# Sparse attention with a maxout layer behind it on one core: the last 136 of 822 tasks in another order

## The chip, the core and the metric

The kernel runs on one core of a Trainium2 chip. The metric is the device time of one execution in microseconds (us); of several executions the median is taken. Three runs of the kernel before gave 164.91, 164.93 and 164.22 us, a median of 164.91 us. A profiled execution stands beside them.

## The reference

Two stages, from float32 inputs to a float32 output of 3072 x 512. Batch is 4, heads 8, sequence 768, head size 64.

```python
# attention: each query sees the keys within 15 positions, and one summary key per block of 32
k_sum = k.reshape(B, H, nb, block, D).max(axis=3)
v_sum = v.reshape(B, H, nb, block, D).mean(axis=3)
scores_l = scale * q @ k^T, masked to |i - j| < 16
scores_s = scale * q @ k_sum^T + log(32)
a = softmax(concat[scores_l, scores_s])
attn = a @ concat[v, v_sum]
# maxout: x is attn as 3072 x 512
out = maximum(x @ w1, x @ w2) @ w_out
```

## The kernel before

The kernel does not compute the maxout in the reference's form. Since max(h1, h2) = h1 + relu(h2 - h1), it computes relu(x @ (w2 - w1)) @ w_out + x @ (w1 @ w_out). The difference of the weights and the product w1 @ w_out are made once.

The work is a list of 822 tasks. A task is one step on one tile: a group of matmuls, an exp, a copy, a load, a store. The program creates the tasks batch by batch; then three strings in `CFG` say everything about their placing. `CFG["engines"]` has one letter for each task: T is TensorE (PE), D is VectorE (DVE), A is ScalarE (ACT), P is GpSimd (POOL), S is the queue of SyncE (SP). `CFG["order"]` is a list of task numbers in the order in which they are emitted, and each engine runs its own tasks in that order. `CFG["slots"]` has one digit for each buffer, which says which tile of its ring it gets. All three are written out by hand or by a search outside the program; `Plan.run` (lines 122 to 132) only reads them. Waits follow from the buffers: a task waits for the writers of what it reads, and for the last users of the tile that it writes into. A store or a copy that waits holds up whatever stands behind it on its engine.

The labels name a task by its numbers, and these are needed to follow the steps:

- "scores", "exp", "mask", "values", "inv", "x" and "dxt" carry batch b, head pair hp (0 or 2) and group grp (0 to 2). "scores 302" is batch 3, head pairs 0 and 1, group 2. "values" has one more digit, the head pair within the two. A group is 256 rows of the sequence.
- "dxt" (lines 595 to 599) is a DMA transpose from SP: it turns the attention output x into the tile xt, from which the maxout reads. "x" (line 590) is the DVE step before it: it divides by the row sum that "inv" (line 587) inverted.
- "hidden" and "relu" (lines 674 to 694) carry b, grp and a quarter n of the hidden layer: eight 256-column matmuls, and the relu behind them on ACT or DVE.
- "outx", "outg0", "outg1", "copy out" and "store" (lines 702 to 733) carry b, grp and a half u of 128 rows. "outx" multiplies xt by w1 @ w_out, "outg0" and "outg1" the halves of the relu's output by w_out, each with four matmuls. Then the tile is copied out of its bank, by ACT or DVE, and stored by the queue of SP or ACT. Tile 320 is cut by columns into 256 + 128 + 128.

A hidden or outx task of batch 3 needs both of its group's transposes, dxt 30g and dxt 32g. The banks of the matmul outputs (eight, ring "banks") are shared by scores, values, hidden and out; a task that takes a bank waits for the step that emptied it.

The output rows of a tile are shifted by 16 (line 727: `at = grp * GT + u * 128 + 16`). So the tile of grp 2, u 1 ends 16 rows beyond its batch, and its last 16 rows are the batch's first: it takes two stores (lines 729 and 731). All other tiles take one.

Before the change, the end of the list is, on the engines that matter:

- PE: values 3200, 3021, 3201, 3020, 3000, 3001; hidden 312, 310, 313, 311; outx 310, outx 311, outg0 311, outx 320 (128), outg1 311; hidden 320, outg0 310, hidden 322, 323, 303, 301, 300, 302, 321; outg1 310, outx and outg0 320 (128), outx and outg0 301, outg1 320 (128), outg1 301, outx and outg0 300, the rest of 320, outg1 300; outx, outg0 and outg1 321.
- DVE, behind mask 300: inv 320, inv 302, x 302, x 320, inv 300, relu 310, 312, 311, x 300, relu 313, copy out 311, relu 300, 322, copy out 310, relu 302, copy out 320 (128) twice.
- ACT, behind exp 301: copy out 211, copy out 221, store 221, exp 302, exp 300, relu 323, store 200, relu 301, store 211, relu 320, 321, 303, copy out 220, copy out 301, store 301, store 311, copy out and store 320 (256), copy out 300, copy out 321, store 321.
- SP, behind the last transpose of keys and queries: store 201, 111, 100, dxt 321, 301, 322, 302, 320, 300, store 011, 210, 310, 220, 121, 320 (128) twice, store 300.

Of the kernel before, what the change touches and what calls it, by code (L numbers as in the profile page):

```python
# [27 lines left out]
DAPAPTADADAPAPDATATDDPDADDTATDDPDPDPSDSDDPDPDSASADDPDTADTTDDSTADTTDDSTADTTDDSTADTTDDSTADTTDDSTADTTDDSSSSDSSSDSSSDSSSDP  # L28
ADPAAATAPPDDDPPAPSASDDDPPASASDDAPPPSDSDDADPDSDSADDPDTADTTDDSTADTTDDSTADTTDDSTADTTDDSTADTTDDSTADTTDDSTTATTDTTATTDTTATTA
TTDTTATTTAATTTASTTDTTDTTATTATTTDSTTTDSTTATTDTTATTDTTTAATTTAATATDTATATTTASTTTASTDTATATDTTTASTTTASTATATDTATTTAATTTASTDTA  # L30
TDTATTTAATTTDSTDTATATATTTDSTTTAATATDTATATTTASTTTAATDTATDTATTTASTTTAATDTDTDTDTTTDSTTTDATATATDTATTTAATTTAATTTDSTTTDS
""".split())
CFG["order"] = list(map(int, """
# [28 lines left out]
""".split()))  # L62
CFG["slots"] = "".join("""
62042222021106710531003202313307231146225:92038;61<0042111340176159:02011300112351100237323242320261022522460324040071
0001000221160432210551<47898;6372010411534153241633000262220121202324610426125432206020144162353<002=47:;8>50241030214
34123211222003301214111422034002204241064003223621;<21536:=01>97125053101142010320204231000000501212040203202124342346
2201623730702125441574016062035031561075120162776743420432132341762015540341624532677725412445001541265304420201127162
""".split())
ENG = {"T": "PE", "D": "DVE", "A": "ACT", "P": "POOL", "S": "SP"}

# [741 lines left out]
```

## Time and profile before

| what | us |
|---|---|
| median of three runs | 164.91 (164.22 to 164.93) |
| the profiled execution's own time | 165.06 |
| its span, first to last instruction | 163.2 |
| PE busy in the span | 152.8 (94%) |
| DVE busy | 111.5 (68%) |
| ACT busy | 97.5 (60%) |

The granted TensorE clock is at full speed throughout. Of the chain of waits that ended last, PE holds 55% of the span, unattributed issue time 15%, DMA 8% and SP's queue 7%. The output stores are 256 KB each. In the rows quoted below, "L715" is the line of the out matmuls, "L678" of the hidden ones, "L690" and "L692" of the relu on ACT and DVE, "L258" of a copy, "L590" of x, "L596" of the transpose, "L729" and "L731" of the two stores. PEld is the weight load of PE, which runs ahead of its matmul. An engine name with a q (SPq, ACTq) is an issue by that engine's queue.

### The profile page before, as it was taken

Reading aid. Unit: us, or ns where it says so; the run is one execution under the profiler, and the core shown is the slowest. Engines: PE = TensorE matmul, PEld = TensorE weight load, DVE = VectorE, ACT = ScalarE, POOL = GpSimd, SP = SyncE. Lnnn points to the kernel's source line nnn. Section 1 sums busy time; section 2 is a strip of 40 time slices with the busy share of each in tenths; the row PEclk is TensorE's granted clock in tenths of the full one; section 3 lists DMA queues with packets and bytes.
Section 4 is the critical chain, followed back from the end, with each engine's and each line's share of the span. In section 5 each row is a group of like instructions: output and inputs, shape, how many; then the busy total and the mean of one; then the engine's idle time right before and its main releaser. Section 6 shows DMA issues by size and latency. Waiting matters only on the chain.

```text
span 163.2 us, 4346 instructions
## 1 busy us (share of the span) xinstructions
PE 152.8 (94%) x1761; PEld 99.9 (61%) x1782; DVE 111.5 (68%) x220; ACT 97.5 (60%) x140; POOL 43.9 (27%) x95
## 2 busy tenths in 40 slices
PE   6977889999999999999999999999999999999990
PEld 2534668888645655588665745868554576686640
DVE  3469999997897899869988576454937967115000
ACT  3369898446529899993999435866659510043121
POOL 6725457003036020069250240000595000000000
PEclk9999999999999999999999999999999999999999
DMA  4999999998999999579899997699996523531752
GB/s 152 324 312 316 263 389 391 395 395 259 281 301 265 308 339 260 89 177 279 114 231 290 320 180 169 120 135 277 229 133 209 128 37 68 161 118 55 233 179 64
DMA packets 67988, 36.48 MB, mean 224 GB/s; under 512 B 54912, under 2 KB 61952, under 8 KB 67968
## 3 DMA queue, kind: packets, MB, share of 16 engines
q1 hardware_dynamic: 66048, 33.43, 77.0%
q10 hardware_dynamic: 1920, 2.77, 5.2%
q8 instruction: 14, 0.23, 0.6%
q14 instruction: 6, 0.05, 0.1%
HBM read 25.18 MB, written 6.29 MB: 193 GB/s over the span
## 4 chain that ended last, share of the span: by engine, by line
PE 55%; issue 15%; DMA 8%; SPq 7%; DVE 6%; POOL 5%; ACT 2%; POOLq 0%; DVEq 0%
PE banks L715 22%; PE banks L678 17%; PE banks L662 4%; SPq L336 4%; DMA land<-in_q_dram 3%; PE banks L569 3%; DMA land<-in_k_dram 3%; POOL vx L256 3%; PE banks L463 3%; PE banks L529 2%; DVE vx L258 2%; POOL kx L258 2%; DVE ks L487 2%; SPq L729 1%; DMA out_dram<-o 1%
## 5 line engine op out<-in xcount | busy, mean ns | idle before, releaser
L678 PE MATMUL banks<-xt,wd 128*128 128x256 bf16 x384 | 45.6, 273 | 0.0
L715 PE MATMUL banks<-wo,g 128*128 128x512 bf16 (+2 forms) x198 | 44.6, 362 | 0.9 <-issue 0.6
L678 PEld LDWEIGHTS <-wd 128*128 128x128 bf16 x384 | 36.9, 98 | 6.9 <-issue 0.3
L715 PEld LDWEIGHTS <-g 128*128 128x128 bf16 x208 | 19.2, 98 | 18.4
L690 ACT ACTIVATE g<-banks 128x512 bf16<-128x512 f32 x28 | 15.7, 596 | 22.2 <-PE banks L678 22.1
L541 ACT ACTIVATE pb<-banks 128x1024 bf16<-128x1024 f32 x24 | 23.7, 1029 | 8.4 <-PE banks L529 8.2
L715 PE MATMUL banks<-w1o,xt 128*128 128x512 bf16 (+2 forms) x96 | 23.6, 362 | 0.6 <-DVE kqb L258 0.2
L692 DVE TENSOR_SCALAR g<-banks 128x512 bf16<-128x512 f32 x20 | 13.5, 685 | 10.4 <-PE banks L678 10.3
L487 DVE TENSOR_REDUCE ks<-kx 128x24 bf16<-128x768 bf16 x16 | 14.9, 947 | 2.7 <-ACT kx L258 2.4
L590 DVE TENSOR_TENSOR xs<-banks,inv 128x512 bf16<-128x512 f32 x24 | 16.4, 689 | 0.5
L258 ACT COPY o<-banks 128x512 f32<-128x512 f32 (+1 forms) x18 | 10.0, 574 | 11.1 <-PE banks L715 7.6
L258 POOL COPY kx<-kx 128x32 bf16<-128x32 bf16 (+1 forms) x16 | 6.5, 422 | 35.9 <-ACT kx L258 20.7
L549 DVE TENSOR_TENSOR pb<-pb,mask 128x1024 bf16<-128x1024 bf16 x18 | 12.2, 693 | 4.3 <-ACT pb L541 4.0
L715 PEld LDWEIGHTS <-xt 128*128 128x128 bf16 x104 | 9.5, 98 | 8.8
L256 POOL COPY vx<-sums 32x396 bf16<-32x396 bf16 x18 | 9.6, 557 | 10.8 <-ACT vx L258 5.5
L750 PE MATMUL banks<-zeros,identity 128*128 128x512 bf16 x29 | 10.3, 465 | 1.6 <-DVE identity L239 1.6
L258 ACT CAST kqb<-land 128x768 bf16<-128x768 f32 x11 | 10.1, 937 | 2.6 <-DMA land<-in_k_dram 2.5
L463 PE MATMUL banks<-ident,kqb 128*128 128x128 f32 x60 | 10.2, 286 | 1.5 <-DVE sums L269 1.1
L258 ACT COPY vx<-vx 32x128 bf16<-32x128 bf16 (+5 forms) x12 | 10.2, 860 | 1.9 <-DVE vx L258 1.7
L463 PEld LDWEIGHTS banks<-ident,kqb 128*128 128x128 f32 x60 | 7.4, 145 | 5.1 <-DVE sums L269 1.5
L258 DVE CAST kqb<-land 128x768 bf16<-128x768 f32 x15 | 8.8, 607 | 2.5 <-DMA land<-in_q_dram 1.3
L258 DVE COPY o<-banks 128x512 f32<-128x512 f32 (+1 forms) x8 | 4.7, 591 | 8.0 <-PE banks L715 6.8
(82 smaller groups left out, 175.7 us busy)
## 6 DMA issues: line engine op xcount, KB each, us to landing
land<-in_k_dram SPq DMA_DIRECT2D x16, 384.0 KB, 5.7
land<-in_v_dram SPq DMA_DIRECT2D x14, 384.0 KB, 5.8
land<-in_q_dram SPq DMA_DIRECT2D x14, 384.0 KB, 5.5
land<-in_moe_w_dram SPq DMA_DIRECT2D x8, 512.0 KB, 8.8
out_dram<-o SPq DMA_DIRECT2D x12, 256.0 KB, 2.6
land<-in_moe_w_out_dram SPq DMA_DIRECT2D x4, 512.0 KB, 11.0
out_dram<-o ACTq DMA_DIRECT2D x7, 256.0 KB, 2.3
w1t<-in_v_dram SPq DMA_DIRECT2D x2, 384.0 KB, 5.3
```

The source lines that it names most:

```text
L256: nc.gpsimd.tensor_copy(out=o[:, n * z:n * z + n], in_=i[:, n * z:n * z + n])
L258: {"D": nc.vector.tensor_copy, "A": nc.scalar.copy, "P": nc.gpsimd.tensor_copy}[e](out=o, in_=i)
L463: nc.tensor.transpose(out=bank(ps)[:, 128 * j:128 * j + 128], in_=src.ap[:].bitcast(F32)[:, 128 * j:128 * j + 128], identity=ident32[:])
L487: op("D", lambda e: nc.vector.tensor_reduce(out=ks.ap[:, 0:nb], in_=free(kt(), 128, [256, NM], [192, 2], [32, 2], [1, 32]), axis=AX.X, op= ...
L541: op("A", lambda e: nc.scalar.activation(out=spread(pb.ap[:, 0, 0:1], [1, 1024]), in_=spread(bank_tile[:, ps.ap, 0:1], [1, 1024]), func=AC ...
L549: on(e).tensor_tensor(out=o.rearrange("p n (u c) -> p n u c", u=2), in0=o.rearrange("p n (u c) -> p n u c", u=2), in1=in1, op=ALU.mult)
L590: op("D", lambda e: nc.vector.tensor_tensor(out=x.ap[:].rearrange("p n u a d -> p n (u a) d"), in0=spread(bank_tile[:, ps.ap, 0:1], [512, ...
L678: nc.tensor.matmul(out=bank(ps)[:, 256 * s:256 * s + 256], lhsT=wd[n // 2][:, c, 256 * (n % 2) + 128 * s:256 * (n % 2) + 128 * s + 128], r ...
L690: nc.scalar.activation(out=o, in_=bank(ps), func=ACT.Relu)
L692: nc.vector.tensor_scalar_max(out=o, in0=bank(ps), scalar1=0.0)
L715: nc.tensor.matmul(out=bank(ps, c1 - c0), lhsT=a, rhs=w, start=(i == j == 0), stop=(i == 2 and j == 3))
L750: nc.tensor.matmul(out=bank(ps), lhsT=identity[:], rhs=zeros[:], start=True, stop=True)
```

## The change

Only the three strings change, and in them only what concerns the last 136 tasks of the order. No task is added or removed. The tile stored last is now 300, whose rows do not wrap.

```diff
 CFG["engines"]
-TDTATTTAATTTDSTDTATATATTTDSTTTAATATDTATATTTASTTTAATDTATDTATTTASTTTAATDTDTDTDTTTDSTTTDATATATDTATTTAATTTAATTTDSTTTDS
+TDTATTTAATTTDSTDTATATATTTDATTTAATATDTATATTTDATTTAATATATATATTTAATTTDATATATATDTTTDSTTTAATATDTATATTTDATTTAATTTDSTTTDS
 CFG["order"]
-521 474 513 481 720 735 747 490 736 522 486 715 491 737 505 753 485 721 685 548 662 564 496 549 532 754 533 550 755
...
-811 802 769 803 770 804 805 806
+521 474 513 481 720 735 747 490 736 522 486 715 491 737 505 753 485 627 721 548 685 564 496 549 532 662 754 703 533
...
+773 766 774 767 775 768 769 770
 CFG["slots"]
-34123211222003301214111422034002204241064003223621;<21536:=01>97125053101142010320204231000000501212040203202124342346
-2201623730702125441574016062035031561075120162776743420432132341762015540341624532677725412445001541265304420201127162
+34123211222003301214111422034002204241064003223621;<21536:=01>97125053101142010320204231000000501213040203202124342246
+2201623730702125441574016062035031561075120162776743420432132341762015540341644032677725532563405261263754430405013312
```

In labels, the end of the list is now:

- PE: values 3200, 3021, 3201, 3001, 3020, 3000; hidden 312, 311, 313; outx 310; hidden 310; outx 320 (128); hidden 321, 323, 322; outx 320 (128); hidden 320; outx 321; the rest of 320 but one outg1; outx 311, hidden 301, outg0 321, hidden 300, outg0 310, hidden 302, outg1 320 (128), outg1 321, outg1 310, hidden 303, outg0 and outg1 311; outx, outg0 and outg1 301; outx, outg0 and outg1 300.
- DVE, behind mask 300: inv 320, inv 302, x 320, x 302, inv 300, copy out 220, x 300, relu 321, 313, copy out 310, copy out 321, copy out 320 (128) twice, copy out 301.
- ACT, behind exp 301: copy out 211, copy out 221, store 221, store 200, exp 302, store 210, exp 300, store 220, relu 312, 311, 323, 322, 320, copy out 320 (256), store 211, relu 310, store 320 (256), relu 300, 302, 301, store 321, relu 303, copy out 311, store 311, store 301, copy out 300, store 300.
- SP, behind the last transpose of keys and queries: store 011, 201, 111, 100, 121, dxt 321, 301, 322, 302, 320, 300, store 310, 320 (128) twice.

Seven steps go from DVE to ACT: relu 300, 302, 310, 311, 312, 322 and copy out 311. Four go from ACT to DVE: relu 321 and copy out 220, 301, 321. Store 210, 220 and 300 go from SP to ACT. Of the slots, xs, o and banks change; relevant are the banks: "outx 320 (256)" takes the bank that hidden 320 had, hidden 310 the one that hidden 312 had, and outx 310 the one that outx 220 had.

8 rows, old and new, of the table turn are left out of this document.

## The prediction

> **What bounds the kernel now.** I read the page first, for the busy shares, then the stretch that the change touches.
>
> ```profile
> PE 152.8 (94%) x1761; PEld 99.9 (61%) x1782; DVE 111.5 (68%) x220; ACT 97.5 (60%) x140; POOL 43.9 (27%) x95
> ```
>
> TensorE (PE) is busy for 94% of the span of 163.2 us. That is an average over stages, so the windows over the end come next; the columns are PE, weight loads, DVE, ACT, POOL, the granted clock, and DMA.
>
> ```profile
> 130.00:135.00 5.00, 4.95 (x78) 3.51 (x77) 3.38 (x8) 1.00 (x2) 0.00 (x0) 1.00 0.37 59
> 140.00:145.00 5.00, 5.00 (x44) 4.10 (x43) 0.69 (x1) 0.60 (x1) 0.00 (x0) 1.00 0.37 141
> 150.00:155.00 5.00, 5.00 (x38) 3.02 (x37) 0.47 (x2) 0.58 (x1) 0.00 (x0) 1.00 0.67 225
> ```
>
> PE is busy for 4.95 to 5.00 of each 5 us, at a granted clock of 1.00. In the last third DVE and ACT mostly wait for PE. So from 130 us on the length is the sum of the matmuls, plus what follows the last of them. The timeline shows what follows.
>
> ```profile
> 157.16 1.89 PE L715 MATMUL banks<-wo,g 128*128 128x512 bf16 x8
> 159.08 0.58 ACT L258 COPY o<-banks 128x512 f32<-128x512 f32 x1 [2.00 <-DMA out_dram<-o]
> 159.70 0.34 ACTq L729 DMA_DIRECT2D out_dram<-o  x1
> 160.08 0.44 ACTq L731 DMA_DIRECT2D out_dram<-o  x1
> ```
>
> The last matmul ends at 159.05 (157.16 + 1.89); the copy of that tile (321) runs from 159.08 to 159.66, and its two stores are issued at 159.70 (112 rows) and 160.08 (the 16 wrapped rows). The copy's wait is put down to a DMA, because an earlier store also ended near 159.08. But PE ended only 0.03 us before the copy began, so PE alone would hold it just as long. How long the stores take is in the table of DMA issues, asked for at 143.6, 159.6 and 160.05 us (KB, then us to landing).
>
> ```profile
> out_dram<-o ACTq DMA_DIRECT2D x1, 256.0 KB, 2.0
> out_dram<-o ACTq DMA_DIRECT2D x1, 224.0 KB, 2.3
> out_dram<-o ACTq DMA_DIRECT2D x1, 32.0 KB, 2.1
> ```
>
> The first is a store of 128 rows alone in its queue. The other two are the end of this kernel: 159.7 + 2.3 = 162.0 and 160.1 + 2.1 = 162.2. Then 1.0 us passes to the end of the span. The execution took 165.06 us, 1.9 more than the span; the three runs have a median of 164.91, 0.15 below it.
>
> **The change, part by part.** *The tail.* Tile 300, stored last now, lies within its batch, so one issue takes the place of two. PE's last matmul, the ACT copy and the ACT issue stay. The landing moves from 162.2 to 159.7 + 2.0 = 161.7 by the row of the 128-row store, or to 162.0 by that of 112 rows. I take the first, since its size and queue are those of the new store: **-0.4 us**, bounds -0.15 and -0.45.
>
> *PE's work.* The matmuls are the same and only their order differs. PE has no idle time left to remove (4.95 to 5.00 above), so the order can only add holes: each wait that it meets is a loss in full. Nothing below zero is to be had here. I follow the waits in the new order.
>
> *Transposes.* The hidden and outx matmuls of the last batch need x transposed, and SP issues that as a DMA. The steps of DVE (x), SP (transpose) and PE (its weight loads, which come just ahead of the matmuls) before the change:
>
> ```profile
> 132.88 1.29 DVE L590 TENSOR_TENSOR xs<-banks,inv 128x512 bf16<-128x512 f32 x2
> 133.60 1.19 SPq L596 DMA_TRANSPOSE xt<-xs  x1
> 132.79 3.39 PEld L678 LDWEIGHTS <-wd 128*128 128x128 bf16 x32
> 136.19 1.50 PEld L715 LDWEIGHTS <-xt 128*128 128x128 bf16 x8
> 137.81 0.74 PEld L715 LDWEIGHTS <-g 128*128 128x128 bf16 x4
> 138.67 0.43 PEld L715 LDWEIGHTS <-xt 128*128 128x128 bf16 x4
> ```
>
> Before, x 302 is the first of the two steps at 132.88, and its transpose is issued at 133.60. After, x 320 goes first, so x 302 ends one step (1.29 / 2 = 0.6 us) later and dxt 302 is issued near 134.2. Who needs it? "outx 320 128", which PE meets at 138.67 before (four hidden tasks, outx 310, outx 311 and outg0 311 stand ahead). After, only four hidden tasks and outx 310 stand ahead: 132.79 + 3.40 (132.79 to 136.19) + 0.86 (137.81 to 138.67) = 137.05. So the transpose is issued 0.6 later and wanted 1.6 earlier. When does it land? The issues at 125.7, 130.4, 133.6 and 104.4 us:
>
> ```profile
> xt<-xs SPq DMA_TRANSPOSE x1, 2.4
> xt<-xs SPq DMA_TRANSPOSE x1, 2.5
> xt<-xs SPq DMA_TRANSPOSE x1, 3.9
> xt<-xs SPq DMA_TRANSPOSE x1, 4.1
> ```
>
> With 2.4 it lands at 136.6, in time; with 3.9 at 138.1, 1.05 late. What makes the difference? The DMA view of 135.5 to 136 and of 105.5 to 106, and the page's line on that queue:
>
> ```profile
> q8 instruction: 1, 0.02, 11.7%
> q8 instruction: 1, 0.02, 19.1%
> q8 instruction: 14, 0.23, 0.6%
> ```
>
> In both slow cases one packet of queue 8 sits on one of the 16 engines that also carry the transpose: 0.117 x 16 x 0.5 = 0.94 us, and 1.5 us. Fourteen such packets against PE's 1761 + 1782 = 3543 instructions make 253 for each, and no other engine has enough instructions for fourteen. So they are taken to be PE's own instruction fetches, placed by PE's position in its stream. That position is the same after the change (some 25 weight loads past 132.79, at 3.39 us for 32), so the fetch comes again near 135.5, this time in the midst of dxt 302's packets, not at their end. Before, dxt 302 landed at 133.6 + 3.9 = 137.5; after, I put it between that and 0.4 us more. PE would wait 0.45 to 0.9; I take **+0.6 us**, with ends 0 (by the 2.4 row) and 1.3 (by the 4.1 row). The cover that hid this before was outx 311 and outg0 311 ahead of it; they are moved to later.
>
> *Stores moved.* Stores 011 and 121 (three issues) now stand ahead of dxt 321 on SP, and 200, 210 and 220 go to ACT.
>
> ```profile
> 121.52 1.83 SPq L729 DMA_DIRECT2D out_dram<-o  x3
> 125.77 1.20 SPq L596 DMA_TRANSPOSE xt<-xs  x1
> 128.69 1.61 SPq L596 DMA_TRANSPOSE xt<-xs  x1
> 127.64 0.44 ACTq L731 DMA_DIRECT2D out_dram<-o  x1
> 128.69 0.69 DVE L258 COPY o<-banks 128x512 f32<-128x512 f32 x1
> xt<-xs SPq DMA_TRANSPOSE x1, 3.3
> GB/s 152 324 312 316 263 389 391 395 395 259 281 301 265 308 339 260 89 177 279 114 231 290 320 180 169 120 135 277 229 133 209 128 37 68 161 118 55 233 179 64
> ```
>
> SP's three issues end at 123.35, and three more at 0.6 each end near 125.2, before the transpose at 125.77: nothing. On ACT, store 200 is issued after store 221 (its second issue ends at 128.1) and store 210 once its tile is copied (128.69 + 0.69 = 129.4), right beside dxt 301, issued at 128.69 and landed 3.3 later at 132.0 (row of the DMA issues). PE needs it at 132.79, so there is 0.8 us of cover. A 256 KB store at the page's best rate of 395 GB/s keeps the engines for 0.66 us. One store is covered, two would cost 0.5. I take **0**, with 0.5 as the upper end.
>
> The Trainium skill, "DMA: Bandwidth & Descriptors", section "Queues, rings and completion order", speaks against this move: a semaphore increment lands only after every earlier write of that DMA engine, across its queues. The 3.3 us above, with store 221 just ahead on ACT's queue, against 2.4 agrees with it; by that rule the transposes pay for each store beside them and the sum is that of rival C.
>
> *New waits on ACT and banks.*
>
> ```profile
> 134.09 0.20 DVE L587 RECIPROCAL inv<-banks 128x8 f32<-128x8 f32 x1
> 143.66 0.60 ACT L690 ACTIVATE g<-banks 128x512 bf16<-128x512 f32 x1 [12.65 <-PE banks L678]
> 148.89 0.69 DVE L258 COPY o<-banks 128x512 f32<-128x512 f32 x1 [1.25 <-PE banks L715]
> ```
>
> Store 220 waits on ACT for copy out 220, which DVE runs after the reciprocal at 134.09, until 134.9; behind it on ACT stands relu 312, which frees the bank of hidden 310. It ends near 134.9 + 0.35 + 0.60 = 135.9 and hidden 310 starts at 136.2: nothing, cover 0.3. Store 321 waits on ACT for copy out 321; relu 303 stands behind it. Two copies (1.4), two issues (0.8) and the relu (0.6) make 2.8 us, while PE has a hidden task and four out steps (4.3) before it needs relu 303: nothing, cover 1.5. "outx 320 256" takes the bank of hidden 320 with only outx 321 (0.86) between: relu 320 starts about 0.35 after the last load of hidden 320 and takes 0.60, so PE may wait 0 to 0.2; I take **+0.1**.
>
> **Sum.** -0.4 + 0.6 + 0 + 0.1 = +0.3 us: 165.06 becomes 165.36, and the runs, 0.15 lower, 165.2.
>
> **Rivals.** *B: only the tail.* If the fetch falls on an engine that has finished, dxt 302 lands after 2.4 and PE never waits: 164.91 - 0.4 = 164.5. For it: undisturbed transposes landed in 2.4 and 2.5, and 136.6 would leave 0.45 us to spare. Against it: both of the transposes above with a fetch among or right behind their packets took 3.9 and 4.1. *C: the stores delay the transposes, and the kernel is slower.* Dxt 301 lands two stores later, at 132.0 + 1.3 = 133.3, and hidden 312 starts 0.5 late; then dxt 302, with store 220 issued near 134.9 beside it, lands 0.4 + 0.66 after 137.5, at 138.6, against PE at 137.05 + 0.5: 1.0 more. The waits make 1.6 with the bank's 0.1, and 164.91 + 1.6 - 0.4 = 166.1. It decides from waits of 0.4 us in all (slower than before) and reaches the 0.5% at 1.2. Against it: the transposes and the stores have separate queues, and most engines would be done with a store in time. That the tile stored last still has wrapped rows can't be: line 727 gives 0 + 0 + 16 as its first row, and 128 rows fit in 768.
>
> **How the numbers follow.** The forecast of 165.2 has 0.47; its own range is 164.9 (tail -0.45, wait 0.45) to 165.9 (tail -0.15, wait 0.9, bank 0.2). B has 0.25, C 0.25; 0.03 is left for what I don't see. Within the range, 164.4 is B less 0.1, and 166.2 is C. The three runs spread from 164.22 to 164.93, so 0.5% (0.8 us) is about what a measurement of this kernel can tell from no change. Faster by that has no mechanism here, since the tail gives 0.45 at most: 0.05 for the spread of the runs. Slower by that needs waits of 1.2, most of C and a little of the forecast: 0.23. Within it: 0.72.
>
> **What would show it.** In the changed profile: one ACT store as the last issue, landing 2.0 us later (else the tail is wrong); a PE gap of some 0.6 us near 137 ahead of a 128-column matmul of L715 on xt, and dxt 302 landing after 137.5, with a queue 8 packet near 135.5 (no gap: B); hidden matmuls starting late, after 132.8, and dxt 301 taking over 4 us (C). A PE gap after 145 would be a chain on ACT or DVE that I took as covered, and would make the prediction wrong in its reasons.

## The result and the profile after

The changed kernel takes 166.23 us (median of 20 runs) against 164.59 us for the kernel before (20 runs). The ratio is 1.0078, with a 95% interval of 1.0051 to 1.0106: slower by 0.8%. (The ratio leaves out runs more than 1.5% above the fastest of their kernel, five of 20 after and two of 20 before, so it is not the quotient of the two medians, and no profile shows what those five runs waited for.) The forecast was 165.2 on a base of 164.91, or +0.3 us; the ratio on that base makes 166.2, or +1.3 us. The sign was right and the size was not: 166.2 lies above the upper end of 165.9 that the forecast gave itself. The fastest of the 20 changed runs, 164.31 us, is as short as a usual run before.

The profiled execution took 166.61 us, with a span of 164.8. I start at the end and go backwards. The timeline of the tail after the change:

```profile
159.26 1.89 PE L715 MATMUL banks<-wo,g 128*128 128x512 bf16 x8
161.18 0.59 ACT L258 COPY o<-banks 128x512 f32<-128x512 f32 x1 [4.50 <-DMA out_dram<-o]
161.80 0.34 ACTq L729 DMA_DIRECT2D out_dram<-o  x1
```

One store is left, and from the start of the last copy to the end of the span it is 164.8 - 161.18 = 3.6 us, where it was 163.2 - 159.08 = 4.1. The tail did what it was given. The loss lies earlier, and the windows show where (PE, weight loads, DVE, ACT, POOL, clock, DMA):

```profile
130.00:135.00 5.00, 4.53 (x76) 3.47 (x75) 4.13 (x9) 1.28 (x3) 0.00 (x0) 1.00 0.41 128
135.00:140.00 5.00, 2.67 (x23) 1.79 (x22) 0.00 (x0) 0.90 (x2) 0.00 (x0) 1.00 0.92 133
140.00:145.00 5.00, 5.00 (x50) 4.17 (x49) 1.29 (x2) 1.79 (x3) 0.00 (x0) 1.00 0.00 0
150.00:155.00 5.00, 5.00 (x36) 3.16 (x35) 1.60 (x4) 1.40 (x3) 0.00 (x0) 1.00 0.02 6
```

PE lost 2.3 us between 135 and 140 and 0.5 just before; from 140 on it is as dense as it was. The timeline shows the large hole, PE's loads and matmuls:

```profile
135.66 0.97 PEld L678 LDWEIGHTS <-wd 128*128 128x128 bf16 x8
139.25 0.23 PEld L715 LDWEIGHTS <-xt 128*128 128x128 bf16 x4 [2.61 <-DMA xt<-xs]
139.25 0.40 PE L715 MATMUL banks<-w1o,xt 128*128 128x128 bf16 x4 [2.33 <-DMA xt<-xs]
```

It is the place that the forecast named: the first outx of 128 columns waits for a transpose, dxt 302. But the hole has 2.3 us, not 0.6. The small hole comes from ACT (the timeline's rows of ACT, its queue, and PE's scores):

```profile
126.39 0.45 ACTq L731 DMA_DIRECT2D out_dram<-o  x1
126.87 2.24 ACTq L729 DMA_DIRECT2D out_dram<-o  x1
127.34 0.68 PE L529 MATMUL banks<-kt,kx 64*128 64x64 bf16 x36
129.16 1.02 ACT L541 ACTIVATE pb<-banks 128x1024 bf16<-128x1024 f32 x1 [3.15 <-issue]
129.24 0.36 ACTq L729 DMA_DIRECT2D out_dram<-o  x1
```

The issue of store 200 keeps ACT's queue for 2.24 us instead of 0.34, and exp 302 stands behind it. Its scores were done at 128.02 (127.34 + 0.68), and it starts at 129.16, 1.1 us late. Part of that comes back as PE's wait for a mask, 0.47 us at 131.88.

To compare stages across executions I use four marks from each timeline: the start of exp 321, the first load of hidden 312, the start of the last copy, the end of the span. Differences are A, B and C.

| kernel | exp 321 | hidden 312 | last copy | span | A | B | C |
|---|---|---|---|---|---|---|---|
| before | 122.05 | 132.79 | 159.08 | 163.16 | 10.74 | 26.29 | 4.08 |
| after | 120.63 | 132.38 | 161.18 | 164.82 | 11.75 | 28.80 | 3.64 |
| e1 | 120.87 | 131.66 | 157.96 | 161.62 | 10.79 | 26.30 | 3.66 |
| e2 | 121.53 | 132.43 | 160.20 | 163.83 | 10.90 | 27.77 | 3.63 |
| e3 | 121.59 | 132.63 | 159.46 | 163.10 | 11.04 | 26.83 | 3.64 |
| e4 | 120.76 | 131.66 | 158.44 | 162.09 | 10.90 | 26.78 | 3.65 |
| e5 | 121.15 | 131.97 | 158.35 | 161.97 | 10.82 | 26.38 | 3.62 |
| e6 | 121.31 | 133.00 | 159.30 | 163.37 | 11.69 | 26.30 | 4.07 |
| e7 | 121.23 | 131.84 | 158.13 | 161.80 | 10.61 | 26.29 | 3.67 |
| e8 | 121.71 | 132.76 | 160.03 | 163.67 | 11.05 | 27.27 | 3.64 |
| e9 | 121.28 | 132.18 | 158.47 | 162.55 | 10.90 | 26.29 | 4.08 |
| e10 | 121.13 | 131.86 | 158.16 | 161.79 | 10.73 | 26.30 | 3.63 |
| e11 | 121.12 | 131.97 | 159.01 | 162.66 | 10.85 | 27.04 | 3.65 |

After the change A is 1.0 longer, B 2.5 longer, C 0.4 shorter: 3.1 us. The span grew by only 1.7, since this execution reached exp 321 1.4 us sooner, ahead of the work that the change moves on PE, DVE and ACT. So the waits of this execution are probably larger than those of the median run.

Why was dxt 302 late? The DMA view at its issue (133.75), and the fetch found in the window 136.4 to 136.5:

```profile
xt<-xs SPq DMA_TRANSPOSE x1, 5.5
q8 instruction: 1, 0.02, 102.5%
```

It took 5.5 us to land, at 139.2. The packet of queue 8, PE's instruction fetch, began between 136.4 and 136.5 and took 1.025 x 16 x 0.1 = 1.64 us, until 138.1. So dxt 302 landed 1.1 us behind the fetch's end. Before the change the same count, in the window 135.5 to 135.6:

```profile
q8 instruction: 1, 0.02, 58.4%
```

0.584 x 16 x 0.1 = 0.93 us, so until 136.5, and the landing came at 133.6 + 3.9 = 137.5, again about 1.1 behind. In both profiles the transpose's data had been moved by then: its 0.13 MB (128 x 512 values of 2 bytes) went over SP's queue between 134.8 and 136.0 after the change, and between 134.7 and 135.5 before. What is held is the landing, not the packets. My theory after the result was: a transpose that has not landed when PE's fetch gets one of its DMA engines lands 1.1 us behind the fetch's end; and a store issue on ACT is held up by such a fetch too. Rival 1: the new PE order alone wants dxt 302 too early. Rival 2: the traffic of the moved stores makes it late, and the fetch has no part.

### The profile page after: what moved, and what is told of

It is laid out like the page before. It is cut to its first block, busy times and chain, and to the rows that moved or that the text cites. A ratio compares the mean times of both kernels' runs of the same rounds, so it can differ in the third digit from the quotient of the medians.

```text
span 164.8 us, 4368 instructions
## 1 busy us (share of the span) xinstructions
PE 154.6 (94%) x1782; PEld 99.5 (60%) x1782; DVE 109.5 (66%) x217; ACT 99.3 (60%) x143; POOL 43.5 (26%) x95
## 4 chain that ended last, share of the span: by engine, by line
PE 76%; DVE 9%; DMA 4%; ACT 4%; ACTq 2%; issue 2%; POOL 1%; POOLq 0%; DVEq 0%
PE banks L715 32%; PE banks L678 24%; PE banks L662 4%; PE banks L569 4%; DMA xt<-xs 3%; PE banks L529 3%; PE banks L463 3%; DVE vx L258 3%; PE banks L750 2%; ACTq L729 2%; DVE ks L487 2%; ACT pb L541 1%; PE banks L639 1%; DMA out_dram<-o 1%; ACT vx L258 1%
## 5 line engine op out<-in xcount | busy, mean ns | idle before, releaser
L678 PE MATMUL banks<-xt,wd 128*128 128x256 bf16 x384 | 46.2, 273 | 0.0
L715 PE MATMUL banks<-wo,g 128*128 128x512 bf16 (+2 forms) x208 | 45.8, 363 | 0.0
L690 ACT ACTIVATE g<-banks 128x512 bf16<-128x512 f32 x33 | 18.8, 597 | 23.5 <-PE banks L678 16.5
L715 PE MATMUL banks<-w1o,xt 128*128 128x512 bf16 (+2 forms) x104 | 24.6, 363 | 2.3 <-DMA xt<-xs 2.3
L692 DVE TENSOR_SCALAR g<-banks 128x512 bf16<-128x512 f32 x15 | 10.1, 685 | 9.6 <-PE banks L678 9.5
L258 DVE COPY o<-banks 128x512 f32<-128x512 f32 (+1 forms) x10 | 5.8, 602 | 15.3 <-PE banks L715 15.2
L258 ACT COPY o<-banks 128x512 f32<-128x512 f32 (+1 forms) x16 | 8.8, 572 | 9.6 <-DMA out_dram<-o 5.6
L256 POOL COPY vx<-sums 32x396 bf16<-32x396 bf16 x18 | 9.0, 528 | 10.1 <-ACT vx L258 5.5
L569 PEld LDWEIGHTS <-pb 128*64 128x64 bf16 x384 | 7.7, 110 | 5.1 <-issue 3.3
L569 PE MATMUL banks<-vx,pb 128*64 128x65 bf16 x384 | 9.6, 196 | 1.1 <-DVE pb L549 0.5
```

The lines of the kernel that those rows point to most:

```text
L258: {"D": nc.vector.tensor_copy, "A": nc.scalar.copy, "P": nc.gpsimd.tensor_copy}[e](out=o, in_=i)
L569: nc.tensor.matmul(out=av(n)[64 * par:64 * par + 64, u, a, :], lhsT=pb.ap[r, at, 64 * par:64 * par + 64], rhs=rhs, start=start, stop=stop)
L678: nc.tensor.matmul(out=bank(ps)[:, 256 * s:256 * s + 256], lhsT=wd[n // 2][:, c, 256 * (n % 2) + 128 * s:256 * (n % 2) + 128 * s + 128], r ...
L690: nc.scalar.activation(out=o, in_=bank(ps), func=ACT.Relu)
L692: nc.vector.tensor_scalar_max(out=o, in0=bank(ps), scalar1=0.0)
L715: nc.tensor.matmul(out=bank(ps, c1 - c0), lhsT=a, rhs=w, start=(i == j == 0), stop=(i == 2 and j == 3))
```

## The experiments

All were timed beside the kernel before on the same chip, each in 12 runs; its median was 164.53 us beside e1 to e4, 164.94 beside e5 to e8 and 164.44 beside e9 to e11. They edit the order with one helper, which puts a task behind another and may give it to another engine:

```python
def _after(task, mark, engine=None):
    order, engines = CFG["order"], list(CFG["engines"])
    order.remove(task)
    order.insert(order.index(mark) + 1, task)
    if engine:
        engines[task] = engine
    CFG["engines"] = "".join(engines)
```

**e1, the tail alone**, on the kernel before: tile 321 goes ahead of outg0 300.

```diff
+for task, mark, engine in ((802, 811, None), (803, 802, None), (804, 803, None), (805, 804, "D"), (806, 805, "S"),
+                           (767, 806, None), (768, 767, None), (769, 768, None), (770, 769, "A")):
+    _after(task, mark, engine)
```

> The kernel before with only the tail changed: the tasks of tile 321 go ahead of outg0 300, so that tile 300 is stored last, by ACT, in one store. All else is as before. Theory (fetch and issue): the tail is worth what the forecast gave it, 0.4 us less (ratio 0.9975), since nothing else moves; in the changed kernel's profile the stretch from the last copy's start to the end of the span shrank from 4.08 to 3.6 us. Rival (the tail is worth nothing, the end being set by something else): ratio 1.000.

Measured: 163.90 us, ratio 0.9961 (0.9926 to 0.9995). C is 3.66, A and B are as before. The tail is worth 0.4 us in the profile, and the interval of the runs (0.1 to 1.2 us) holds that. This version beats both kernels.

**e2, stores 200, 210 and 220 on SP behind dxt 300**, on the changed kernel.

```diff
+for task, mark, engine in ((716, 531, "S"), (734, 716, "S"), (752, 734, "S")):
+    _after(task, mark, engine)
```

> The changed kernel with stores 200, 210 and 220 issued by SP behind dxt 300, so that ACT issues no store between the transposes. Theory (a store issue on ACT is held up while an instruction fetch of PE occupies a DMA engine, and the exps stand behind it; dxt 302's landing is held up by the next fetch): exp 302 starts right behind its scores again and PE's waits for the masks (0.58 + 0.10 us before values 3020) go; some wait for dxt 302 stays, since the fetch stays, 0.5 to 1.5 us instead of 2.6; ratio 1.000 to 1.004. Rival 1 (PE's new order alone wants dxt 302 too early): PE's wait at the first outx of 128 columns stays above 2 us, ratio 1.005 or more. Rival 2 (the traffic of these stores makes the transposes late, the fetch has no part): dxt 302 lands 2.4 us after its issue, PE doesn't wait, ratio 0.9975.

Measured: 165.35 us, ratio 1.0058 (1.0025 to 1.0090). A falls to 10.90: the exps are on time. Of B's loss 1.5 us stays. PE's wait, and the DMA view at the issue (133.80) and of 136.2 to 136.3:

```profile
138.26 0.40 PE L715 MATMUL banks<-w1o,xt 128*128 128x128 bf16 x4 [1.30 <-DMA xt<-xs]
```

```profile
xt<-xs SPq DMA_TRANSPOSE x1, 4.4
q8 instruction: 1, 0.02, 58.2%
```

The fetch takes 0.93 us with no store beside it, so it ends near 137.15; the landing is at 133.8 + 4.4 = 138.2, 1.1 us behind. Rival 2 falls as the whole cause: without any of these stores the transpose is still late. But it lands 4.4 us after its issue instead of 5.5, so they have a part in it. The ratio lies above what I expected; rival 1 is still open.

**e3, stores 200 and 210 on ACT but behind exp 300.**

```diff
+for task, mark, engine in ((716, 525, None), (734, 716, None)):
+    _after(task, mark, engine)
```

> The changed kernel with stores 200 and 210 still on ACT, but behind exp 300, so that no exp stands behind a store issue; store 220 follows as before. Theory (fetch and issue): the exps are on time and PE's waits for the masks go (some 1.0 us of the profile); the wait for dxt 302 stays, with three stores in its neighbourhood 1.5 to 3 us; ratio 1.002 to 1.006. Rival 1 (order alone): nothing changes, 1.008. Rival 2 (traffic alone): more traffic beside dxt 302, as late as before or later, 1.008 or more.

Measured: 164.84 us, ratio 1.0024 (0.9992 to 1.0056). A is 11.04, so the exps are no longer held; PE waits 0.36 us for dxt 302, less than I expected. In this profile the fetch began late, at 137.3. Dxt 302 landed 0.2 us behind its start, after 3.5 us, so the hold did not come. It took 1 us more than an undisturbed transpose all the same: store 220 was issued 0.7 us behind it, and dxt 302 landed 0.2 us behind that store.

**e4, PE's fetches shifted**, on the changed kernel: the fillers at the start are cut in two.

```diff
-            nc.tensor.matmul(out=bank(ps), lhsT=identity[:], rhs=zeros[:], start=True, stop=True)
+            for _ in range(2):
+                nc.tensor.matmul(out=bank(ps, 256), lhsT=identity[:], rhs=zeros[:, 0:256], start=True, stop=True)
```

> The changed kernel, with each of the 30 filler matmuls at the start (128x512 on zeros, nobody reads them) cut into two of 256 columns: the same PE time, but 60 more instructions, so that all later fetches of PE's instructions come 60 instructions (some 3.3 us in the hidden stretch) earlier against the work. Nothing else changes. Theory (fetch and issue): the fetch that lay beside dxt 302 comes some 3 us sooner, when hidden 312 begins; dxt 302 lands 2.4 to 3 us after its issue, PE waits there 0 to 0.5 us instead of 2.6; if the fetch before it also moves clear of store 200 on ACT, the exps are on time; ratio 0.997 to 1.003. Rivals 1 and 2 (order alone, traffic alone): the fetch has no part, so the wait for dxt 302 stays above 2 us and the ratio at 1.008.

Measured: 164.13 us, ratio 0.9992 (0.9959 to 1.0026). Sixty more instructions, which compute nothing new, take the whole loss away. The fetch lies between 132.5 and 132.6 now, 0.9 us past hidden 312 instead of 4.1; B falls from 28.80 to 26.78. Both rivals expected 1.008. That the fetch moved with PE's instruction count also shows that queue 8 is PE's. A small wait is left, with no fetch beside the transpose (the DMA view at its issue, 133.04, and PE):

```profile
xt<-xs SPq DMA_TRANSPOSE x1, 3.4
136.50 0.40 PE L715 MATMUL banks<-w1o,xt 128*128 128x128 bf16 x4 [0.31 <-DMA xt<-xs]
```

Store 220 is again issued 0.7 us behind dxt 302, and dxt 302 lands 0.2 us behind it.

**e5, x 302 first**, on top of e2, with a swap of banks 2 and 4 so that hidden 311 takes the banks that x 302 frees.

```diff
+_after(538, 562)
+slots = list(CFG["slots"])
+for buffer, digit in ((448, "2"), (454, "4"), (459, "2"), (463, "2"), (471, "4")):
+    slots[buffer] = digit
+CFG["slots"] = "".join(slots)
```

> The kernel of run e2 (the changed kernel with stores 200, 210 and 220 behind the transposes on SP), and x 302 goes ahead of x 320 on DVE again, as before the change; hidden 311 takes the banks that x 302 frees, and four later tasks swap banks 2 and 4 with it. Theory (fetch and issue): what counts is whether dxt 302 is through before PE's fetch gets its DMA engine. In e2 its packets were through 0.3 us ahead of the fetch and the landing was still held to 1.08 us behind the fetch's end. Issued 0.6 us sooner it lands after 2.4 to 2.6 us, at about the time when the fetch begins; PE's wait of 1.5 us goes wholly: ratio 0.996 to 0.999. If the landing is held all the same, it stays at 1.08 us behind the fetch's end and nothing is gained: 1.005. Rival (lateness adds up: 0.6 us sooner is 0.6 us gained): PE's wait falls to about 0.9, ratio 1.002.

Measured: 164.21 us, ratio 0.9961 (0.9927 to 0.9994). The issues at 132.92 (dxt 302) and 134.21 (dxt 320), and the fetch between 135.3 and 135.4:

```profile
xt<-xs SPq DMA_TRANSPOSE x1, 2.4
q8 instruction: 1, 0.02, 103.4%
xt<-xs SPq DMA_TRANSPOSE x1, 4.4
```

Issued 0.95 us past hidden 312 (132.92 - 131.97) instead of 1.37 in e2, dxt 302 lands at 135.3, just as the fetch begins, and PE has no hole at all: 1.3 us of waiting go for 0.4. The next transpose now has the hold: dxt 320 takes 4.4 us, but nobody wants it yet. So it is a cliff, as the theory said, not lateness that adds up. Two things differ from e2: dxt 320 landed 1.6 us behind the fetch's end, not 1.1, and the fetch took 1.65 us (1.034 x 16 x 0.1), although no store was beside it here either.

**e6, stores 200 and 210 early on ACT, alone**, on the kernel before.

```diff
+for task, mark, engine in ((716, 757, None), (734, 557, "A")):
+    _after(task, mark, engine)
```

> The kernel before with one part of the change alone: ACT issues store 200 behind store 221, ahead of exp 302, and store 210 between exp 302 and exp 300. Theory (fetch and issue): the issue of store 200 is held up by PE's fetch near 128 us, exp 302 starts about 1 us late and PE waits for a mask: from exp 321 to hidden 312 11.3 to 11.8 us instead of 10.73; the wait for dxt 302 does not come, since PE wants it late here: ratio 1.003 to 1.006. Rival 1 (PE's order alone): 1.000.

Measured: 164.80 us, ratio 0.9996 (0.9963 to 1.0030). The profile shows the mechanism, with A at 11.69 (the rows of ACT):

```profile
127.58 2.28 ACTq L729 DMA_DIRECT2D out_dram<-o  x1
129.91 1.02 ACT L541 ACTIVATE pb<-banks 128x1024 bf16<-128x1024 f32 x1 [3.20 <-DMA out_dram<-o]
```

But the median of the runs doesn't have it, and the expectation of 1.003 to 1.006 is not met. In e8, with the same two stores early, the issue took 1.67 us and A was 11.05. The hold of an ACT issue is shown in these three profiles (after, e6, e8). The kernels with cut fillers show it too: there the fetch comes earlier (126.3 to 127.0), and it is the second issue of store 221 that takes 1.3 to 1.7 us (e4, e7, e9, e10). In all seven the held issue ends 0.3 to 0.4 us behind the fetch. What it costs in a usual run is under 0.3%.

**e7, e2 and e4 together.** The edits are those of e2 and e4.

> The kernel of run e2 with the cut fillers of run e4: no store beside the transposes, and PE's fetch some 3 us earlier against the work. Theory (fetch and issue): dxt 302 meets neither and lands 2.4 to 2.6 us after its issue, PE doesn't wait: 26.3 to 26.5 us from hidden 312 to the last copy, ratio 0.996 to 0.998. Rival 1 (PE's order wants dxt 302 too early by itself): some 1.5 us of waiting as in e2, ratio 1.005.

Measured: 163.59 us, ratio 0.9932 (0.9902 to 0.9963). PE has no hole (B is 26.29), and each of the last three transposes took 2.4 to 2.5 us. With the changed PE order untouched, nothing is lost: rival 1 falls, and this version beats both kernels as well. The ratio is below the 0.996 to 0.998 that I expected, but the interval reaches 0.996.

Four of the profiles make a square that separates the fetch from the store (the wait is that of PE's weight loads):

| kernel | fetch before dxt 302 has landed | store 220 beside it | dxt 302, issue to landing | PE's loads wait |
|---|---|---|---|---|
| after | yes | yes | 5.5 | 2.6 |
| e2 | yes | no | 4.4 | 1.6 |
| e4 | no | yes | 3.4 | 0.6 |
| e7 | no | no | 2.4 | 0 |

By the landing the fetch is worth 2.0 us and the store 1.0, each with and without the other; of PE's wait it is 1.6 to 2.0 and 0.6 to 1.0. So rival 2 has the smaller part of the loss right. (E2 and e7 move stores 200 and 210 as well, but in the other two these had landed before dxt 302 was issued.) Each row is one execution.

**e8, store 220 alone on SP behind dxt 300.**

```diff
+_after(752, 531, "S")
```

> The changed kernel with store 220 alone taken away from ACT, to SP behind dxt 300; stores 200 and 210 stay ahead of the exps. Theory (fetch and issue): the exps stay 1 us late (11.5 to 11.8 us from exp 321 to hidden 312); the fetch beside dxt 302 has no store to share its engine with and takes 0.93 us instead of 1.64, so PE waits 1.0 to 1.6 us instead of 2.6; ratio 1.005 to 1.007. Rival 2 (store 220's traffic is what makes dxt 302 late): no wait, ratio 1.003 or less.

Measured: 165.24 us, ratio 1.0023 (0.9988 to 1.0057). The hole stays, as in e2:

```profile
138.10 0.40 PE L715 MATMUL banks<-w1o,xt 128*128 128x128 bf16 x4 [0.81 <-DMA xt<-xs]
```

The fetch (59.4% of a window of 0.1 us at 136.0, so 0.95 us) and the wait (1.1 us by PE's loads) are as I expected, the ratio is below. The reason that I gave for the fetch's length, a store that shares its engine, does not hold: see e5. That e8 should be faster than e2, which takes more stores out of the way, I can't explain; the intervals overlap.

**e9, the cut fillers on the kernel before**, the control for e4 and e7.

> The kernel before with the cut fillers of runs e4 and e7 and nothing else: the control for both. Theory (the cut only moves PE's fetches, and the kernel before waits for no transpose that a fetch holds): 26.3 us from hidden 312 to the last copy as before, ratio 0.998 to 1.001. Rival (the cut saves time by itself, at the start or elsewhere): ratio 0.997 or less, and the gains of e4 and e7 are partly that.

Measured: 163.92 us, ratio 0.9986 (0.9951 to 1.0021), B 26.29. The cut does nothing that these runs can tell.

**e10, e1 with the cut fillers.**

> The kernel of run e1 (the kernel before, tile 300 stored last) with the cut fillers. Theory: the tail's gain alone, as in e1: 0.995 to 0.998. Rival (the cut saves time by itself): 0.992 to 0.994, as fast as e7.

Measured: 163.71 us, ratio 0.9962 (0.9923 to 1.0001), the same as e1. The kernel before had no hole to take away.

**e11, x 302 first with the stores where the change put them.** The edit is that of e5 alone.

> The changed kernel with x 302 ahead of x 320 and the bank swap of run e5, but with its stores 200, 210 and 220 on ACT where the change put them. Theory (what decides is whether dxt 302 is through before the fetch): issued 0.6 us sooner it is through, and PE's wait at the first outx of 128 columns falls from 2.6 to under 0.5 us; the exps may stay late behind store 200; ratio 0.997 to 1.002. Rival (the stores beside the transposes are needed for the loss to go): a wait of more than 1 us stays, ratio 1.004 or more.

Measured: 164.13 us, ratio 0.9988 (0.9950 to 1.0026). Dxt 302 takes 2.4 us and its hole is gone. Another one shows up: the DMA view at 127.75 (dxt 301), and PE at hidden 312:

```profile
xt<-xs SPq DMA_TRANSPOSE x1, 4.9
```

```profile
132.73 1.03 PE L678 MATMUL banks<-xt,wd 128*128 128x256 bf16 x8 [0.69 <-DMA xt<-xs]
```

Dxt 301, with stores 200 and 210 on ACT's queue beside it, landed at 132.7, 0.2 us behind store 210, and hidden 312 waited 0.7 us. That is the first half of the forecast's rival C, in an execution in which it did come.

## Why the prediction was right in sign and too small

**PE as the bound: right.** Wherever PE had no wait, B is 26.29 to 26.38 us: in seven kernels, with the order of before and with the changed one (e5, e7). The order could only add holes.

**The tail, -0.4: right.** 4.08 to 3.64 us in the profile; e1 has it alone. (162.2 - 161.7 is 0.5 by the rounded rows; I took 0.4.)

**The wait at the first outx of 128 columns, +0.6: right place, wrong size.** It was 2.6 us by PE's loads. This is the term that failed, in the step that PE's position in its stream "is the same after the change (some 25 weight loads past 132.79), so the fetch comes again near 135.5", and that the landing is the old one plus at most 0.4. Four things were off:

- The fetch began 4.1 us past hidden 312 instead of 2.75. Outx 310 now lies ahead of it, whose four loads take 0.86 us where four of a hidden task take 0.43. In e5 and e8, with the same PE order, it began 3.4 and 3.3 us past hidden 312, in e3 4.7. Why it varies so much is not settled.
- It took 1.64 us instead of 0.93. Why is not settled either: e5's took 1.65 with no store beside it, e7's 1.36 with no other packet beside it.
- The landing follows the fetch's end by 1.1 us, and I had expected the fetch in the midst of dxt 302's packets, with the landing 0.4 us later at most. 138.1 + 1.1 against 136.63, when PE was ready, is the wait of 2.6 us of the loads.
- Store 220 beside dxt 302 had no price in this term; by the square above it is worth 1.0 us. In the changed profile an undisturbed dxt 302 would have landed at 133.75 + 2.4 = 136.15, ahead of the fetch at 136.5. That the store is what kept it open until then is argued, not shown.

The upper end that I gave (1.3) was the 4.1 row. The trace of before has a slower transpose of this form that I had not looked at: the one issued at 93.3 us took 4.7 us to land. By it the upper end would have been 134.2 + 4.7 - 137.05 = 1.9. And the range of 164.9 to 165.9 used 0.9 for this wait and nothing for the stores, though I had given 1.3 and 0.5 as their ends; with these it would have reached 166.8.

**Stores on ACT, 0: wrong.** I priced the traffic and the slack of the tasks behind each store, and took an issue at 0.34 us throughout. An issue of 2.24 us next to a fetch was not in the sum, though SP's issue of 2.03 us at 134.90 before the change showed the like. In the profile A is 1.0 longer, of which PE's wait for a mask is 0.5 and the rest is not placed; in the runs it costs less, by e6.

**The bank of outx 320 (256), +0.1: not seen.** PE's only waits past 121 us are those above. The covered waits on ACT (store 220, store 321) stayed covered.

**The rivals.** B, only the tail, gave 164.5, and the three fastest runs of the changed kernel (164.31 to 164.59) agree with that, but none of them was profiled. C named a slower result of 166.1 by way of the stores; the time agrees with the runs, the way only in part: its delay of dxt 301 came in e11, while hidden 312 had no wait in the changed kernel's profile. Dxt 302 was held by the fetch with store 220 beside it and without (e2, e8), but the 1.0 us that C gave that store is what the square shows. The Trainium skill, "DMA: Bandwidth & Descriptors", section "Queues, rings and completion order", says that a semaphore increment lands only after every earlier write of that DMA engine, across its queues. The traces agree where a store is beside: dxt 302 landed 0.2 us behind store 220 after the change and in e3 and e4. In e2 and e8 there was no store, and the landing stood behind an instruction fetch. That it is the same ordering which makes the 1.1 us is argued, not shown.

**The chances.** Slower by over 0.5% had 0.23 and is what came, against 0.72 for no change beyond 0.5%. I had rows of both mechanisms, but priced the first in the middle of the rows that I used and the second not at all.

**What stays open.** How often a fetch meets dxt 302 in runs that were not profiled; what sets the fetch's start and length; and why e2, e3 and e8 differ, with one profile for each.

## What to carry to other kernels

Where PE is dense, a new order of the same matmuls can only lose, so price every transfer that it wants earlier by the slowest row of its kind in the whole trace, not by the usual one. Look for PE's instruction fetches among the DMA packets, and keep a transfer on which PE waits clear of them, or early enough to be through: here 0.4 us in the issue of one transpose (e11), or 60 instructions at the start (e4), made up for the whole loss, within what the runs can tell. Keep a large store from being issued right behind such a transfer (1.0 us of its landing here, e7 against e4). And don't put a store issue ahead of work on a computing engine where a fetch may hold it.

## What the runs showed of the hardware

- PE's instructions came as 14 packets of 16 KB (0.23 MB / 14) on a queue of their own, which the profile counts on the same 16 DMA engines as the data. One took 0.9 us in most cases and up to 2.1 us (e10, at 83.4 us). Other traffic does not explain which: 0.93 us in e2 among a transpose's packets, 1.36 us in e7 with no other packet beside it.
- Dxt 302, not yet landed when such a fetch began, landed 1.0 to 1.1 us behind the fetch's end, in the profiles of before, after, e1, e2, e6 and e8 alike. Dxt 320 in its place landed 1.6 us behind (e5) and 0.7 (e11). Without a fetch or a store close by, the transpose took 2.4 to 2.5 us (e5, e7, e11); with a store issued 0.7 us behind it, 3.4 to 3.5 (e3, e4).
- An issue on the queue of ACT or SP, some 0.3 to 0.6 us for a store and 1.2 us for a transpose when free, took 1.1 to 2.3 us (store) and up to 2.7 us (dxt 300 after the change) when it fell into a fetch.

The last is the row of SP's queue after the change, in the fetch from 136.4 to 138.1:

```profile
136.47 2.71 SPq L596 DMA_TRANSPOSE xt<-xs  x1
```
